# Hedgehog feature maps: min - x formed on GpSimd from x - max, and three value tiles with their constant columns set once

## The chip, the cores and the metric

The kernel runs on one core of a Trainium2 chip. The metric is the device time of one execution in microseconds (us); lower is better. The profile and the text use short names for the engines of the core: PE is TensorE (matmul), DVE is VectorE, ACT is ScalarE, POOL is GpSimd and SP is SyncE, which issues most DMAs.

## The reference

Four residual layers alternate, an ordinary attention (A) and a linear attention with "Hedgehog" features (B): A, B, A, B, on 2048 tokens of width 512, with 32 heads of 16. The part that matters here is B:

```python
pq = jnp.einsum("bhsd,hdf->bhsf", q, w_phi)
pk = jnp.einsum("bhsd,hdf->bhsf", k, w_phi)
phi_q = jnp.concatenate([_softmax(pq, axis=-1), _softmax(-pq, axis=-1)], axis=-1)
phi_k = jnp.concatenate([_softmax(pk, axis=-1), _softmax(-pk, axis=-1)], axis=-1)
kv = jnp.einsum("bhsf,bhsd->bhfd", phi_k, v)
z  = jnp.einsum("bhsf->bhf", phi_k)
num = jnp.einsum("bhqf,bhfd->bhqd", phi_q, kv)
den = jnp.einsum("bhqf,bhf->bhq", phi_q, z)[..., None] + 1e-6
o = num / den
```

For each token and head there are two softmaxes over 16 numbers, one of x and one of -x. A softmax of x is computed from x - max, one of -x from min - x.

## The kernel before, in words

The two A layers (`LayerA`) run their attention as one long sequence of PE, ACT and PE steps: scores (L877), exp (L880) and the product with the values (L891). Other work is put between them by a hand-written schedule (`pump`), in pieces of a generator.

The two B layers (`LayerB`) begin with `feed`, which goes over the 2048 tokens in 16 tiles of 128: `feed(j, ...)` is called for j = 0 to 3 and does four tiles each time; tt counts the tiles from 0 to 15. For each tile PE projects k's features into a PSUM bank (`pk`), q's into another (`pq`), and the values into a third (`pbv`), with 12 matmuls each (L1064). Three banks of the pool `psS` are there; one holds the sum of phi_k times v (`kvp`), so the three projections of a tile share two banks in turn, and each has to wait until the readers of the bank before it are done.

The steps of a tile after the projections, in the order in which the code issues them:

- `expo(pk)`: max (L1124) and min (L1125) over 16 numbers on DVE, then x - max (L1127) and min - x (L1128) on DVE into the two sides of `f`, 128 x 1024 numbers, then one exp on ACT (L1129). `expo(pq)` does the same for q.
- the values are copied to the high part of `vt` on ACT (L1097);
- `share` of k: the sums of 16 exps (L1135), the reciprocal (L1136) and a scale (L1138) on DVE, then the product on POOL (L1144); the low part of the values on DVE (L1092); `share` of q: L1135, L1136 and L1144, without a scale;
- `halves` of k: a high part in f16 on ACT (L1150), the low part on POOL (L1151).

Two things are done one tile later, in the middle of PE's projections of the next tile: `turn` transposes q's features on PE (L1175), and ACT copies them out (L1176); `gather` multiplies phi_k with the values on PE (L1182). The value tile `vt` holds, for two parts and 32 heads, 16 values and a seventeenth column with a constant: 1 in the high part, which makes the normalizer z, and 0 in the low part. It comes from a pool of five buffers (`yn`), and two memsets on POOL (L1068, L1069) set the constant columns for each tile.

During the first tiles `between` (a call to `pumps`) lets leftovers of the A layer run: the output projection of the last block of tokens (L585, L573), its layer statistics (L389 to L423, of which L396 and L397 are on DVE and L406 to L423, fourteen short steps, on POOL) and its transposition (L446 to L459). The memset L710 prepares a row for the next attention.

The order on all four compute engines in `feed` is the order of the code: it runs under `tc.manual_schedule(engines=COMPUTE)`, and each engine takes its instructions in that order. A wait at the head of an engine's queue holds up everything behind it. The last tile (tt = 15) goes another way at its end (`share_split`, `blocks`), and `rest` and `finish` follow with the outputs of the layer.

Of the kernel before, what the change touches and what calls it, by code (L numbers as in the profile page):

```python
# [10 lines left out]
F16 = mybir.dt.float16  # L11
# [3 lines left out]
ALU = mybir.AluOpType  # L15
AX = mybir.AxisListType

P = 128
S = 2048
D = 512  # L20
H = 32
DH = 16
# [28 lines left out]
def mha_hedgehog_stack(ctx, tc, x_in, a_wqkv, a_wo, b_wqkv, b_wphi, b_wo, out, shmin=SHMIN):  # L51
    nc = tc.nc
# [7 lines left out]
    np_ = pool("np", bufs=2)  # L60
# [5 lines left out]
    def big(shape, dt, name):  # L66
        return bigp.tile(shape, dt, tag="big", name=name)
# [306 lines left out]
    class Norm:  # L374
# [83 lines left out]
        def low(self, t, n, ps):  # L458
            nc.vector.tensor_tensor(self.part(1, t, n), ps.rearrange("p u (c x) -> p c u x", c=NC4), self.part(0, t, n), ALU.subtract)  # L459
# [156 lines left out]
    class LayerA:  # L616
# [4 lines left out]
        def begin(self, w0=None):  # L621
            self.start_octet(0, w0 or self.octet_w(0))
# [173 lines left out]
        def feed(self, lns, work):  # L796

            for j, (a, b, c) in enumerate(work):
                ln = lns[j]
                self.xnT.append(ln.xnT)  # L800
                ln.turn01()
                a()
                ln.turn23()
                b()
                c()
                if j == 2:
                    self.head_norms(0)
                self.head(j)
                if j == 2:
                    self.next_w = self.octet_w(1)  # L810
                    self.load_head()
                if 0 < j < NJ - 1:
                    self.head_values(j - 1)
            self.feed_end()
# [220 lines left out]
    class LayerB:  # L1035
# [3 lines left out]
        def begin(self):  # L1039
            self.wqk = stgp.tile([P, 2, 2, NC4, 512], F16, tag="stg", name="wbqk")  # L1040
            nc.sync.dma_start(self.wqk, dBqk)
            self.wv = []
            for a in range(2):
                t = wp.tile([P, NC4, 512], F16, tag="w", name=f"wbv{a}")
                nc.sync.dma_start(t, dBv[a])
                self.wv.append(t)
            self.kvp = None
            self.latek = self.lateq = None
            self.qT, self.obs = [], []

        def feed(self, j, xnT, between=lambda t: None):

            if self.kvp is None:
                self.kvp = psS.tile([P, 2, 512], F32, tag="S", name="kvp")
            qT = [big([P, 4, 512], F32, f"qT{j}_{i}") for i in range(2)]
            self.qT.append(qT)
            for t in range(4):
                tt = 4 * j + t

                def project(dst, w, passes=(0, 1, 2)):  # L1060
                    for i in passes:
                        a, b = PASSES[i]
                        for c in range(NC4):
                            nc.tensor.matmul(dst, xnT[:, a, c, t * P:(t + 1) * P], w(b, c),  # L1064
                                             start=(i == 0 and c == 0), stop=(i == 2 and c == NC4 - 1))

                vt = np_.tile([P, 2, H, 17], F16, tag="yn", name="vt", bufs=5)
                nc.gpsimd.memset(vt[:, 0, :, 16:17], 1.0)  # L1068
                nc.gpsimd.memset(vt[:, 1, :, 16:17], 0.0)  # L1069
                bank = lambda name: psS.tile([P, 2, 512], F32, tag="S", name=name)[:, 0, :]  # L1070
                last = tt == NT - 1
                pk = bank("pk")
                project(pk, lambda b, c: self.wqk[:, 1, b, c, :])
                if last:
                    f_k = self.expo(pk)
                    self.kvb = [np_.tile([P, 4, P], F32, tag="yn", name="kvb", bufs=5) for _ in range(2)]
                    for kvb in self.kvb:
                        nc.gpsimd.memset(kvb, 0.0)
                else:
                    pq = bank("pq")  # L1080
                    project(pq, lambda b, c: self.wqk[:, 0, b, c, :])
                if self.lateq is not None and tt < NT - 2:
                    self.turn(*self.lateq)
                pv_ = bank("pbv")
                project(pv_, lambda b, c: self.wv[b][:, c, :])
                if self.latek is not None:
                    self.gather(*self.latek)
                if last:
                    pq = bank("pq")
                    project(pq, lambda b, c: self.wqk[:, 0, b, c, :], (0, 1))  # L1090
                pvh = pv_.rearrange("p (h d) -> p h d", d=DH)
                low = lambda: nc.vector.scalar_tensor_tensor(  # L1092
                    vt[:, 1, :, 0:16], pvh, 2.0 ** -8, vt[:, 0, :, 0:16], op0=ALU.mult, op1=ALU.subtract)
                if not last:
                    f_k = self.expo(pk)
                    f_q = self.expo(pq)
                nc.scalar.activation(vt[:, 0, :, 0:16], pvh, AF.Copy, scale=2.0 ** -8)  # L1097
                if last:
                    fk = self.share_split(f_k, low)
                    self.turn(*self.todo)  # L1100
                    self.gather(tt, fk, vt)
                    project(pq, lambda b, c: self.wqk[:, 0, b, c, :], (2,))
                    self.blocks()
                    self.todo = [self.lateq, (tt, self.expo(pq), qT)]
                    for q in self.todo:
                        self.share(q[1], 1.0)
                    return
                self.share(f_k, KS)
                low()
                if tt == NT - 2:  # L1110
                    self.todo = self.lateq
                    self.latek = (tt, self.halves(f_k), vt)
                else:
                    self.share(f_q, 1.0)
                    self.latek = (tt, self.halves(f_k), vt)
                self.lateq = (tt, f_q, qT)
                between(tt)

        def expo(self, ps):

            pf = ps.rearrange("p (h f) -> p h f", f=DH)
            mx = sp.tile([P, H], F32, name="mx")
            mn = sp.tile([P, H], F32, name="mn")
            nc.vector.tensor_reduce(mx, pf, AX.X, ALU.max)  # L1124
            nc.vector.tensor_reduce(mn, pf, AX.X, ALU.min)  # L1125
            f = pp.tile([P, H, 2, DH], F32, tag="p", name="f")
            nc.vector.tensor_tensor(f[:, :, 0, :], pf, mx.unsqueeze(2).to_broadcast([P, H, DH]), ALU.subtract)  # L1127
            nc.vector.tensor_tensor(f[:, :, 1, :], mn.unsqueeze(2).to_broadcast([P, H, DH]), pf, ALU.subtract)  # L1128
            nc.scalar.activation(f, f, AF.Exp, scale=con["pB"])  # L1129
            return f  # L1130

# [270 lines left out]
```

## Time and profile before

| | us |
|---|---|
| median of 3 runs | 2550.31 |
| lowest and highest of them | 2549.44, 2551.63 |
| the profiled execution | 2549.26 |
| its span, from the first to the last instruction | 2547.5 |

| engine | busy us | share of the span | instructions |
|---|---|---|---|
| PE | 2447.8 | 96% | 20960 |
| DVE | 974.0 | 38% | 1884 |
| ACT | 2177.5 | 85% | 2437 |
| POOL | 379.0 | 15% | 523 |

The shares are means over very different stages. The feature stage of the first B layer lies at about 1043 to 1215 us of the span and that of the second at about 2293 to 2465 us; between them and before them lie the two attention layers. The granted PE clock was 0.99 over the span.

In the rows of the profile, a group of instructions has its source line, the engine, the operation, what it writes and reads, and how often it occurs; behind the bar stand its busy time, the mean ns of one, and the idle time of its engine in front of it with what ended that. Rows in order of time start with the start and the duration in us; a bracket at the end gives the idle time before the first instruction of the row and what ended it.

### The profile page before, as it was taken

What the parts mean: (1) busy time and instruction counts of PE and PEld (TensorE: products, weight loads), DVE (VectorE), ACT (ScalarE), POOL (GpSimd) and SP (SyncE); (2) the same over time, 40 slices, a digit from 0 to 9 for tenths busy, and PEclk for the clock granted to TensorE, in tenths of its full rate; (3) what the DMA queues carried; (4) which work ended last, traced back from release to release, by engine and by line L of the source; (5) the groups of instructions that cost most, each with busy time, mean ns of one, the idle gap of its engine ahead of it and who ended that gap; (6) DMA issues with size and microseconds to landing.
All of it is one profiled execution on the core that took longest, in us unless ns stands there. A gap on an engine that the chain in (4) does not pass through costs nothing.

```text
span 2547.5 us, 50724 instructions
## 1 busy us (share of the span) xinstructions
PE 2447.8 (96%) x20960; PEld 761.2 (30%) x20960; DVE 974.0 (38%) x1884; ACT 2177.5 (85%) x2437; POOL 379.0 (15%) x523
## 2 busy tenths in 40 slices
PE   6799999999999999999899999999999999998998
PEld 3222222222232222345343222222222222224543
DVE  6212211212133316899871122112122111459897
ACT  5699999999999999644438999999999999993552
POOL 2100000101000000266430010000010000005552
PEclk9899999999999999999999999999999999999999
DMA  3510230033033612100224003202300351110003
GB/s 141 104 44 5 43 47 6 14 50 78 1 79 66 222 51 84 50 17 6 70 96 68 14 6 50 40 1 45 65 2 10 71 140 41 67 67 26 9 17 109
DMA packets 109650, 135.29 MB, mean 53 GB/s; under 512 B 63408, under 2 KB 64672, under 8 KB 107232
## 3 DMA queue, kind: packets, MB, share of 16 engines
q1 hardware_dynamic: 108736, 129.59, 20.7%
q8 instruction: 166, 2.72, 0.4%
q0 software_dynamic: 672, 2.36, 0.2%
q14 instruction: 76, 0.62, 0.1%
HBM read 60.06 MB, written 39.85 MB: 39 GB/s over the span
## 4 chain that ended last, share of the span: by engine, by line
PE 78%; DVE 11%; ACT 5%; issue 3%; POOL 2%; SPq 1%; DMA 0%; ACTq 0%; POOLq 0%; DVEq 0%
PE pv L891 37%; PE s L877 21%; PE pqk L585 6%; PE po L585 5%; ACT p L880 3%; DVE su L1135 2%; PE pbv L1064 1%; PE pk L1064 1%; PE pq L1064 1%; DVE f L1127 1%; POOL f L1144 1%; DVE f L1128 1%; DVE mx L1124 1%; PE pst L446 1%; DVE su L1136 1%
## 5 line engine op out<-in xcount | busy, mean ns | idle before, releaser
L880 ACT ACTIVATE p<-s 128x1024 f32<-128x1024 f32 x2048 | 1887.8, 1116 | 20.2 <-PE s L877 17.7
L891 PE MATMUL pv<-p,v 128*32 128x512 f32 x8192 | 1091.9, 605 | 2.6 <-DVE yt L503 1.8
L877 PE MATMUL s<-kq 49*128 49x512 f16 x3872 | 606.1, 382 | 20.3 <-DMA kq<-sh 12.0
L877 PEld LDWEIGHTS <-kq 49*128 49x128 f16 x3968 | 136.8, 94 | 637.4 <-issue 625.3
L891 PEld LDWEIGHTS pv<-p,v 128*32 128x32 f32 x8192 | 161.8, 108 | 397.3 <-issue 367.2
L687 POOL TENSOR_TENSOR sq<-stg 128x512 bf16<-128x512 f16 x48 | 70.1, 1460 | 1043.1 <-DVE stg L761 940.2
L503 DVE STREAM_TRANSPOSE yt<-pv 128x512 f32<-128x512 f32 x64 | 45.8, 716 | 452.9 <-PE pv L891 441.0
L760 DVE TENSOR_SCALAR tq<-pqk,c_qk 128x512 f32<-128x512 f32 x48 | 35.9, 749 | 445.0 <-PE pqk L585 411.8
L1144 POOL TENSOR_TENSOR f<-f,su 128x1024 f32<-128x1024 f32 x62 | 119.8, 1933 | 386.0 <-DVE su L1138 351.6
L1064 PEld LDWEIGHTS <-xnTa 128*128 128x128 f16 x1152 | 110.6, 99 | 150.8 <-DVE f L1128 23.6
L585 PEld LDWEIGHTS <-wA 128*32 128x32 f16 (+1 forms) x2496 | 86.6, 97 | 200.8 <-issue 175.2
L573 DVE SCALAR_TENSOR_TENSOR xt<-po,c_oA,xt 128x512 f32<-128x512 f32 x64 | 47.1, 735 | 233.9 <-PE po L585 223.5
L585 PE MATMUL pqk<-xnTb,wA 128*32 128x512 f16 (+1 forms) x1248 | 116.9, 379 | 2.2 <-ACT xnTb L456 2.2
L585 PE MATMUL pqk<-xnT,wA 128*32 128x512 f16 (+1 forms) x1224 | 110.9, 379 | 3.1 <-ACT xnT L456 2.5
L1064 PE MATMUL pbv<-wbv,xnTa 128*128 128x512 f16 x384 | 92.9, 394 | 19.0 <-DVE f L1128 19.0
L1129 ACT ACTIVATE f<-f,c_pB 128x1024 f32<-128x1024 f32 x64 | 72.7, 1148 | 42.3 <-DVE f L1128 42.2
L1150 ACT ACTIVATE fk<-f 128x1024 f16<-128x1024 f32 x30 | 31.7, 1057 | 73.6 <-POOL f L1144 73.6
L585 PE MATMUL po<-woA,ob 128*32 128x512 f16 x1152 | 92.3, 379 | 0.0
L1064 PE MATMUL pk<-wbqk,xnTa 128*128 128x512 f16 x384 | 88.5, 379 | 0.0
L1064 PE MATMUL pq<-wbqk,xnTa 128*128 128x512 f16 x384 | 88.4, 379 | 0.0
L1135 DVE TENSOR_REDUCE su<-f 128x64 f32<-128x1024 f32 x64 | 77.5, 1211 | 9.2 <-ACT f L1129 8.5
L1176 ACT ACTIVATE qT<-pqt 128x512 f32<-128x512 f32 x64 | 34.6, 593 | 52.0 <-PE pqt L1175 52.0
(280 smaller groups left out, 1930.1 us busy)
## 6 DMA issues: line engine op xcount, KB each, us to landing
kq<-stg SPq DMA_DIRECT2D x168, 128.0 KB
xd<-xt SPq DMA_DIRECT2D x40, 512.0 KB
xt<-xd SPq DMA_DIRECT2D x40, 512.0 KB
v<-vyt SPq DMA_DIRECT2D x384, 16.0 KB
oD<-osp SPq DMA_DIRECT2D x24, 256.0 KB
ob<-oD SPq DMA_DIRECT2D x8, 768.0 KB
xt<-in_A_x_dram SPq DMA_DIRECT2D x8, 512.0 KB
wbqk<-dBqk SPq DMA_DIRECT2D x2, 2048.0 KB
```

The source lines that it names most:

```text
L503: nc.vector.transpose(yt.rearrange("p a b -> p (a b)"), ps)
L573: nc.vector.scalar_tensor_tensor(xt[:, u, :], ps, co, xt[:, u, :], op0=ALU.mult, op1=ALU.add)
L585: nc.tensor.matmul(ps[r, :], w[:, r], x, start=(n == 0), stop=(n == of - 1), skip_group_check=cols)
L687: nc.gpsimd.tensor_tensor(sq, hi, hi, ALU.mult)
L760: nc.vector.tensor_scalar(tq, ps, cqk, CLAMP, op0=ALU.mult, op1=ALU.min)
L877: nc.tensor.matmul(s[:, u, :], self.side(g, half, r, 0, kt * P, P), self.side(g, half, r, 1, j * 512, 512), start=True, stop=True)
L880: nc.scalar.activation(pt, s, AF.Exp, scale=0.25 / (QS * QS))
L891: nc.tensor.matmul(acc[32 * hh:32 * hh + 32, :], self.oct[o]["v"][:, r:r + 32], pt[:, hh % 2, :], start=(kt == 0), stop=(kt == NT - 1), sk ...
L1064: nc.tensor.matmul(dst, xnT[:, a, c, t * P:(t + 1) * P], w(b, c), start=(i == 0 and c == 0), stop=(i == 2 and c == NC4 - 1))
L1129: nc.scalar.activation(f, f, AF.Exp, scale=con["pB"])
L1135: nc.vector.tensor_reduce(su, f[:, r, :], AX.X, ALU.add)
L1144: nc.gpsimd.tensor_tensor(f3, f3, self.part_sums(f3, slice(0, 64), factor), ALU.mult)
```

## The change

In `expo`, the step min - x no longer reads PSUM on DVE. POOL first forms min - max (32 numbers per partition) and then (min - max) - (x - max), which is min - x, from the side of `f` that DVE has just written. DVE keeps max, min and x - max. In `feed`, three value tiles are made in the first three tiles of tokens, with the constant columns set there, and used in turn by the others.

```diff
-            self.qT, self.obs = [], []
+            self.qT, self.obs, self.vts = [], [], []
...
-                vt = np_.tile([P, 2, H, 17], F16, tag="yn", name="vt", bufs=5)
-                nc.gpsimd.memset(vt[:, 0, :, 16:17], 1.0)
-                nc.gpsimd.memset(vt[:, 1, :, 16:17], 0.0)
+                if tt < 3:
+                    self.vts.append(np_.tile([P, 2, H, 17], F16, tag="yn", name="vt", bufs=5))
+                    nc.gpsimd.memset(self.vts[tt][:, 0, :, 16:17], 1.0)
+                    nc.gpsimd.memset(self.vts[tt][:, 1, :, 16:17], 0.0)
+                vt = self.vts[tt % 3]
...
             nc.vector.tensor_tensor(f[:, :, 0, :], pf, mx.unsqueeze(2).to_broadcast([P, H, DH]), ALU.subtract)
-            nc.vector.tensor_tensor(f[:, :, 1, :], mn.unsqueeze(2).to_broadcast([P, H, DH]), pf, ALU.subtract)
+            nc.gpsimd.tensor_tensor(mn, mn, mx, ALU.subtract)
+            nc.gpsimd.tensor_tensor(f[:, :, 1, :], mn.unsqueeze(2).to_broadcast([P, H, DH]), f[:, :, 0, :], ALU.subtract)
             nc.scalar.activation(f, f, AF.Exp, scale=con["pB"])
```

## The prediction

> **What bounds the kernel now.** I read the page from the top: the engines' shares, then the chain that ended last, then the feature stage alone, first in stretches and then instruction by instruction.
>
> ```profile
> span 2547.5 us, 50724 instructions
> PE 2447.8 (96%) x20960; PEld 761.2 (30%) x20960; DVE 974.0 (38%) x1884; ACT 2177.5 (85%) x2437; POOL 379.0 (15%) x523
> PE pv L891 37%; PE s L877 21%; PE pqk L585 6%; PE po L585 5%; ACT p L880 3%; DVE su L1135 2%; PE pbv L1064 1%; PE pk L1064 1%; PE pq L1064 1%; DVE f L1127 1%; POOL f L1144 1%; DVE f L1128 1%; DVE mx L1124 1%; PE pst L446 1%; DVE su L1136 1%
> ```
>
> TensorE carries the whole kernel, and L891 and L877 of the chain, its two attention layers, hold none of the changed lines. VectorE (DVE; L1135, L1127, L1128, L1124) and GpSimd (POOL; L1144) reach the chain only in the feature stage, which runs twice, over 16 tiles of 128 tokens each time. So I look there. Two stretches of it, one with side work (a tile with leftovers of the attention layer) and one quiet; columns are PE, weight loads, DVE, ACT, POOL busy time, clock, DMA share and GB/s:
>
> ```profile
> 1142.00:1153.00 11.00, 10.03 (x72) 5.59 (x72) 9.52 (x16) 5.31 (x8) 6.16 (x6) 1.00 0.01 1
> 1182.20:1191.60 9.40, 9.40 (x69) 5.13 (x68) 9.08 (x15) 4.78 (x7) 6.29 (x6) 1.00 0.01 2
> ```
>
> In the quiet tile PE is busy for 9.40 of 9.40 us; DVE is close to full; POOL has 3.1 us free. In the other tile nobody is full. The order in time says why. A quiet tile (k and q are the two halves of a tile's features):
>
> ```profile
> 1179.07 1.93 POOL L1144 TENSOR_TENSOR f<-f,su 128x1024 f32<-128x1024 f32 x1 [0.40 <-DVE su L1136]
> 1180.96 2.14 POOL L1151 TENSOR_TENSOR fk<-f,fk 128x1024 f16<-128x1024 f32 x1
> 1181.16 1.04 PE L1175 MATMUL pqt<-ident,f 128*128 128x128 f32 x8
> 1181.80 1.08 ACT L1176 ACTIVATE qT<-pqt 128x512 f32<-128x512 f32 x2 [2.03 <-PE pqt L1175]
> 1182.77 2.26 ACT L1129 ACTIVATE f<-f,c_pB 128x1024 f32<-128x1024 f32 x2
> 1183.95 1.22 DVE L1135 TENSOR_REDUCE su<-f 128x64 f32<-128x1024 f32 x1
> 1186.13 1.94 POOL L1144 TENSOR_TENSOR f<-f,su 128x1024 f32<-128x1024 f32 x1 [2.71 <-DVE su L1138]
> 1188.47 1.94 POOL L1144 TENSOR_TENSOR f<-f,su 128x1024 f32<-128x1024 f32 x1 [0.40 <-DVE su L1136]
> 1190.36 2.13 POOL L1151 TENSOR_TENSOR fk<-f,fk 128x1024 f16<-128x1024 f32 x1
> ```
>
> This is a ring from one q share on POOL (1179.07, L1144) to the next (1188.47), 9.40 us. The share's end (1181.00) lets PE transpose it (L1175), ACT copies the transposes out (L1176), and only behind them in ACT's queue stands the next tile's exp of k (1182.77); then the sums (L1135) and k's share, q's sums and q's share. The PE transposes start when PE has finished its projection, so PE and this ring are both nearly tight. Note POOL at 1180.96: it forms the low part of k (L1151) right behind q's share, until 1183.10, and its reader, PE's gather, comes later still.
>
> A tile with side work has pieces of both layers on DVE:
>
> ```profile
> 1142.47 2.76 PE L1064 MATMUL pbv<-wbv,xnTa 128*128 128x512 f16 x12 [1.07 <-DVE f L1128]
> 1153.58 2.76 PE L1064 MATMUL pbv<-wbv,xnTa 128*128 128x512 f16 x12 [1.07 <-DVE f L1128]
> ```
>
> Its period is 11.11 us, and PE waits 1.07 us for DVE's L1128, the last reader of the PSUM bank that PE wants.
>
> **The change, part by part.** The prices first: POOL's rows, the DVE row that goes, and two DVE steps that follow one another.
>
> ```profile
> L1144 POOL TENSOR_TENSOR f<-f,su 128x1024 f32<-128x1024 f32 x62 | 119.8, 1933 | 386.0 <-DVE su L1138 351.6 <-DVE su L1136 28.5 <-PE po L585 5.9
> L687 POOL TENSOR_TENSOR sq<-stg 128x512 bf16<-128x512 f16 x48 | 70.1, 1460 | 1043.1 <-DVE stg L761 940.2 <-DVE rec L505 102.9
> L523 POOL TENSOR_TENSOR obB<-yb,obB 128x512 f16<-128x512 f32 x32 | 37.2, 1162 | 68.2 <-ACT obB L522 68.2
> L1069 POOL MEMSET vt<- 128x32 f16 x32 | 10.3, 321 | 0.0
> L1068 POOL MEMSET vt<- 128x32 f16 x32 | 7.6, 239 | 98.3 <-DVE yb L518 98.3
> L710 POOL MEMSET sh<- 1x512 f16 x12 | 6.2, 514 | 175.4 <-PE po L585 161.2 <-DMA kqe<-sh 11.4 <-DMA kq<-sh 2.8
> L1128 DVE TENSOR_TENSOR f<-mn,pk 128x512 f32<-128x512 f32 x16 | 10.8, 677 | 0.0
> 1189.37 0.68 DVE L1127 TENSOR_TENSOR f<-pk,mx 128x512 f32<-128x512 f32 x1
> 1189.96 0.68 DVE L1128 TENSOR_TENSOR f<-mn,pk 128x512 f32<-128x512 f32 x1
> ```
>
> Removed from DVE: one L1128 per half, 64 in all. It lasts 677 ns, but consecutive steps start 0.59 us apart (1189.37, 1189.96), so a tile's two halves free 1.2 us of DVE. The bank of PSUM is also freed 0.6 us sooner. The constant columns: 52 of the 64 memsets (239 and 321 ns) go; they lie in POOL's idle time, nobody waits for them, so by themselves they are worth nothing. The reuse of three value tiles adds no wait that matters: tile t writes a buffer whose last reader, the gather of tile t-3, ran two tiles earlier.
>
> Added on POOL, per half: a 128x32 subtraction, and a 128x512 f32 subtraction. No row shows the latter. From below it is half of L1144's 1933 ns, 0.97 us; from above L687's 1.46 us, which has the element count but 16-bit types; L523 has 1.16. I take 1.06: L1144 is the same type and engine, and 0.19 us of it, the time of a nearly empty POOL step (1070.86, next fence), does not halve: (1.93 - 0.19)/2 + 0.19. The Trainium skill's "GPSIMD Engine Reference", section 3.1, has 4497 ns for a two-input f32 step of 2048 elements, so by estimate 1.12 for 512; the sum would grow by 1.7 us. Section 4.1 of that page of the Trainium skill speaks against the change outright: elementwise two-input work belongs on VectorE, GpSimd being about twice as slow; the rows here agree (1.06 by 0.68). For the small one I look at POOL's short steps behind a statistics step:
>
> ```profile
> 1068.63 2.13 POOL L1151 TENSOR_TENSOR fk<-f,fk 128x1024 f16<-128x1024 f32 x1
> 1068.79 2.00 DVE L397 TENSOR_SCALAR ly<-lu 128x2 int32<-128x2 int32 x1
> 1070.86 0.19 POOL L406 TENSOR_TENSOR lu<-ly 128x2 f32<-128x2 f32 x1
> 1074.39 0.20 POOL L423 TENSOR_TENSOR lb<-lu,ly 128x2 f32<-128x2 f32 x1
> ```
>
> From L406 to L423 are 14 short steps, each waiting for the one before: 3.53/13 = 0.27 us a step. That is the small subtraction's price (128x2 here, 128x32 there; 0.27 to 0.33). The same fence shows an oddity: L397, a two-column DVE step, took 2.00 us and ended as POOL's L1151 did (1070.79 and 1070.76). The Trainium skill's "GPSIMD Engine Reference", section 8, says that the two engines share their SBUF interfaces and contend when DVE runs in a two-port mode or has two SBUF inputs; this row agrees. In a quiet tile the one DVE step of L397's kind (a number times a column in SBUF) is the scaling of k's sums, for which POOL will stand idle, so no term follows from it; in front of the statistics L397 ends with the low part before and after the change.
>
> What decides is where POOL's new work stands. In the changed program POOL's order per tile is: small and large subtraction of k, of q, then k's share, q's share, k's low part. GpSimd takes them in that order. So tile t+1's subtraction of k is queued behind q's share and k's low part of tile t, and ACT's exp, DVE's sums, k's share wait behind it. The low part, which held nobody up, enters the ring:
>
> q's share to the low part's start 1190.36 - 1188.47 = 1.89; low part 2.13; small 0.27; large 1.06; to ACT 0.04; exp of k to the next q share 1188.47 - 1182.77 = 5.70. Sum 11.09 us per tile, against 9.40 in a quiet tile and 11.11 in one with side work. PE's own 9.40 fits under it; DVE's 1.2 us become idle time in front of L1135.
>
> Now one layer, from q's share of tile 0 to that of tile 9 and of tile 13:
>
> ```profile
> 1057.14 1.93 POOL L1144 TENSOR_TENSOR f<-f,su 128x1024 f32<-128x1024 f32 x1 [0.36 <-DVE su L1136]
> 1160.34 1.93 POOL L1144 TENSOR_TENSOR f<-f,su 128x1024 f32<-128x1024 f32 x1 [0.40 <-DVE su L1136]
> 1197.86 1.94 POOL L1144 TENSOR_TENSOR f<-f,su 128x1024 f32<-128x1024 f32 x1 [0.40 <-DVE su L1136]
> 1204.71 1.93 POOL L1144 TENSOR_TENSOR f<-f,su 128x1024 f32<-128x1024 f32 x1 [2.52 <-DVE su L1138]
> 1207.81 2.13 POOL L1151 TENSOR_TENSOR fk<-f,fk 128x1024 f16<-128x1024 f32 x1 [1.17 <-ACT fk L1150]
> 1208.74 1.15 ACT L1129 ACTIVATE f<-f,c_pB 128x1024 f32<-128x1024 f32 x1 [1.01 <-DVE f L1128]
> ```
>
> The first nine periods take 103.20 us, the last four 37.52 (9.38 each). After: four quiet ones are 44.36, so +6.8. The first nine are 99.8, plus what POOL must do in between: twice the statistics (3.53 + 0.20 = 3.73, ahead of k's subtraction in the queue), two pairs of memsets that stay (0.24 + 0.32 each; the third pair runs before the stage), and one L710 (0.51): 108.9, so +5.7. Tile 14's k share then stands 5.39 + (1186.13 - 1182.77 = 3.36) = 8.75 behind q's share of tile 13 instead of 6.85: +1.9. In tile 15 the exp (1208.74) would wait for the low part of tile 14 (until 1209.94) and the two subtractions: 1209.94 + 0.27 + 1.06 + 0.04 = 1211.31, +2.6; part of it is covered by PE's projection and the gather behind it, and in the stage behind, where DVE ends last, the last L1128 gives back 0.6. I take half of 2.6 less 0.6, +0.7, of 0 to 2.6. Per layer 6.8 + 5.7 + 1.9 + 0.7 = 15.1; twice, as both layers run the same program, 30.2.
>
> The profiled execution took 2549.26 us, 1.8 more than its span, and 1.05 less than the median of 2550.31. 2549.26 + 30.2 + 1.05 = 2580.5: I forecast 2580.
>
> **The rivals.** *Faster, 2532 us.* By sums POOL has room: 6.29 busy of 9.40, plus 2 x 1.33, less 0.56 of memsets, is 8.4. Were the new steps hidden so, DVE's 1.2 us would count where PE waits for L1128 (1.07 us in the tile with side work): nine tiles, twice, 1.0 each, -18. It holds if k's subtraction gets onto POOL before tile t-1's low part. The queue's order says no; it would take shares that finish earlier than now, and the q share is itself at the end of the DVE work. 5%.
>
> *No change, 2550.* The early tiles gain what the quiet ones lose: 6.8 a layer over nine tiles, 0.75 each. It needs the ring to be 10.3 us where there is side work, so a subtraction at 0.3 us; nothing in the rows is that cheap. 3%.
>
> *Dearer, 2591 to 2602.* The large step reads and writes every other run of 16 numbers, and could cost like L687, 1.46. The ring grows by 0.40 per tile if only k's step is in it: 28 x 0.40 = 11, 2591; up to 22, 2602, if q's step delays its exp and through ACT's queue the low step of the values. 12%.
>
> **How the numbers follow.** The likeliest case has 80%. Its lower end takes 0.97 for the large step (-0.09 in each of 14 periods a layer, -2.5) and nothing for tile 15 (-1.4), 2576; a little more for a ring that closes tighter than my sum, 2570. The upper end takes most of the dearer case, 2600. A measurement of this kernel can tell some 0.2%, 5 us, from no change. Slower by more than that is 92%, within it 3%, faster 5%.
>
> **What would show it.** In the changed profile quiet tiles should have q shares 11.1 us apart; ACT's exp should be released by POOL, not DVE; PE should wait for POOL or for DVE's sums; DVE's idle time in front of L1135 should grow; the new 128x512 row should read 1.0 to 1.2 us; POOL should be nearly without gaps from q's share to the next subtraction of k. I am wrong if quiet tiles stay at 9.4 us, or if exp starts before the low part of the tile before has ended.

## The result and the profile after

The changed kernel takes 2586.05 us (median of 4 runs, 2584.79 to 2588.74), the kernel before in the same session 2549.88 (4 runs, 2547.28 to 2551.63): 36.2 us more, a ratio of 1.0144 [1.0132, 1.0156]. The forecast was 2580, with a range of 2570 to 2600. The profiled execution took 2586.64, its span 2584.9.

I read the page again from the top. The span, the engines and the chain that ended last, of the changed kernel (the last line is the chain's, by engine and line):

```profile
span 2584.9 us, 50771 instructions
PE 2458.9 (95%) x20960; PEld 763.1 (30%) x20960; DVE 937.7 (36%) x1820; ACT 2181.8 (84%) x2437; POOL 451.9 (17%) x599
PE pv L891 37%; PE s L877 20%; PE pqk L585 5%; PE po L585 5%; ACT p L880 3%; DVE su L1138 3%; POOL f L1147 2%; POOL fk L1154 2%; ACT f L1132 1%; DVE su L1139 1%; POOL f L1131 1%; PE pn L1207 1%; PE pst L446 1%; DVE vt L1094 1%; DVE st L389 1%
```

DVE has 36.3 us less to do and POOL 72.9 more, 64 + 64 steps against 52 memsets fewer. The chain now names POOL three times: L1147 (the share; L1144 before, then 1%), L1154 (the low part of k; L1151 before, not in the list then) and the new L1131.

The prices, from the groups of POOL's instructions (count, then busy time and mean ns of one, then the idle time before and who ended it):

```profile
L1131 POOL TENSOR_TENSOR f<-mn,f 128x512 f32<-128x512 f32 x64 | 67.7, 1058 | 7.2 <-DVE f L1129 2.5
L1130 POOL TENSOR_TENSOR mn<-mn,mx 128x32 f32<-128x32 f32 x64 | 16.2, 253 | 258.0 <-DVE mn L1127 257.7
```

The large step takes 1058 ns where 1.06 us was forecast, the small one 253 ns. Now a quiet tile, in order of time, from one q share on POOL to the next:

```profile
1177.10 1.93 POOL L1147 TENSOR_TENSOR f<-f,su 128x1024 f32<-128x1024 f32 x1 [0.38 <-DVE su L1139]
1178.99 2.14 POOL L1154 TENSOR_TENSOR fk<-f,fk 128x1024 f16<-128x1024 f32 x1
1179.09 1.09 PE L1178 MATMUL pqt<-ident,f 128*128 128x128 f32 x8 [1.04 <-POOL f L1147]
1181.08 0.25 POOL L1130 TENSOR_TENSOR mn<-mn,mx 128x32 f32<-128x32 f32 x1
1181.41 1.06 POOL L1131 TENSOR_TENSOR f<-mn,f 128x512 f32<-128x512 f32 x1
1182.50 1.15 ACT L1132 ACTIVATE f<-f,c_pB 128x1024 f32<-128x1024 f32 x1 [1.64 <-POOL f L1131]
1183.69 1.22 DVE L1138 TENSOR_REDUCE su<-f 128x64 f32<-128x1024 f32 x1 [3.20 <-ACT f L1132]
1185.87 1.94 POOL L1147 TENSOR_TENSOR f<-f,su 128x1024 f32<-128x1024 f32 x1 [2.05 <-DVE su L1141]
1188.18 1.93 POOL L1147 TENSOR_TENSOR f<-f,su 128x1024 f32<-128x1024 f32 x1 [0.37 <-DVE su L1139]
```

1188.18 - 1177.10 = 11.08 us, against 9.40 before. POOL runs without a gap from q's share (1177.10) through the low part (1178.99), the small step (1181.08) and the large one (1181.41); ACT's exp of k waits 1.64 us for exactly that last step, and DVE's sums wait 3.20 us for the exp where they came without a wait before. POOL has its only long gap, 2.05 us, in front of k's share (1185.87), where it stands waiting for DVE. PE waits 1.04 us for the q share (1179.09). The same period in PE, weight loads, DVE, ACT and POOL busy time, clock, DMA share, GB/s:

```profile
1177.10:1188.18 11.08, 9.77 (x70) 5.09 (x69) 7.77 (x13) 4.92 (x7) 8.50 (x8) 1.00 0.00 1
```

PE is no longer full in a quiet tile (9.77 of 11.08), DVE has 7.77 and POOL 8.50. No engine is full: the loop over the four engines is the bound. So every sign that the prediction named is there.

How much of the 36 us lies where is read from the share rows, here those at which the sections of a layer begin and end (tile 0's k share and q share, the q shares of tiles 9 and 13, tile 14's k share, the last share; then the first and last of the second layer), first after, then those of before that have not been shown:

```profile
1054.70 1.94 POOL L1147 TENSOR_TENSOR f<-f,su 128x1024 f32<-128x1024 f32 x1 [1.51 <-DVE su L1141]
1057.44 1.93 POOL L1147 TENSOR_TENSOR f<-f,su 128x1024 f32<-128x1024 f32 x1 [0.80 <-DVE su L1139]
1166.01 1.93 POOL L1147 TENSOR_TENSOR f<-f,su 128x1024 f32<-128x1024 f32 x1 [0.38 <-DVE su L1139]
1210.34 1.93 POOL L1147 TENSOR_TENSOR f<-f,su 128x1024 f32<-128x1024 f32 x1 [0.38 <-DVE su L1139]
1219.11 1.93 POOL L1147 TENSOR_TENSOR f<-f,su 128x1024 f32<-128x1024 f32 x1 [2.05 <-DVE su L1141]
1243.01 1.93 POOL L1147 TENSOR_TENSOR f<-f,su 128x1024 f32<-128x1024 f32 x1 [1.77 <-DVE su L1139]
2323.67 1.94 POOL L1147 TENSOR_TENSOR f<-f,su 128x1024 f32<-128x1024 f32 x1 [1.51 <-DVE su L1141]
2512.18 1.93 POOL L1147 TENSOR_TENSOR f<-f,su 128x1024 f32<-128x1024 f32 x1 [1.77 <-DVE su L1139]
```

```profile
1054.84 1.94 POOL L1144 TENSOR_TENSOR f<-f,su 128x1024 f32<-128x1024 f32 x1 [18.50 <-DVE su L1138]
1225.82 1.93 POOL L1144 TENSOR_TENSOR f<-f,su 128x1024 f32<-128x1024 f32 x1 [1.78 <-DVE su L1136]
2304.80 1.93 POOL L1144 TENSOR_TENSOR f<-f,su 128x1024 f32<-128x1024 f32 x1 [242.72 <-DVE su L1138]
2474.79 1.93 POOL L1144 TENSOR_TENSOR f<-f,su 128x1024 f32<-128x1024 f32 x1 [1.78 <-DVE su L1136]
```

| part of a layer, us | before, layer 1 / 2 | after, layer 1 / 2 | difference | forecast |
|---|---|---|---|---|
| k share to q share of tile 0 | 2.30 / 2.30 | 2.74 / 2.75 | +0.44 / +0.45 | none |
| first nine periods | 103.20 / 102.20 | 108.57 / 108.54 | +5.37 / +6.34 | +5.7 |
| last four periods | 37.52 / 37.52 | 44.33 / 44.32 | +6.81 / +6.80 | +6.8 |
| to tile 14's k share | 6.85 / 6.86 | 8.77 / 8.77 | +1.92 / +1.91 | +1.9 |
| from there to the last share | 21.11 / 21.11 | 23.90 / 24.13 | +2.79 / +3.02 | +0.7 |
| the layer | 170.98 / 169.99 | 188.31 / 188.51 | +17.33 / +18.52 | +15.1 |

The two layers hold 35.85 of the 37.4 us by which the spans differ. Of the rest, 1.68 lie between the layers, where nothing changed; over the kernels below, this stretch varies between 1078.3 and 1082.3 us without any order that follows the edits, so I don't put it down to the change.

### The profile page after: what moved, and what is told of

It reads as the page before. It is cut to its first block, busy times and chain, and to the rows that moved or that the text cites. A ratio compares the mean times of both kernels' runs of the same rounds, so it can differ in the third digit from the quotient of the medians.

```text
span 2584.9 us, 50771 instructions
## 1 busy us (share of the span) xinstructions
PE 2458.9 (95%) x20960; PEld 763.1 (30%) x20960; DVE 937.7 (36%) x1820; ACT 2181.8 (84%) x2437; POOL 451.9 (17%) x599
## 4 chain that ended last, share of the span: by engine, by line
PE 73%; DVE 11%; POOL 6%; ACT 6%; issue 3%; SPq 1%; DMA 0%; POOLq 0%; ACTq 0%; DVEq 0%
PE pv L891 37%; PE s L877 20%; PE pqk L585 5%; PE po L585 5%; ACT p L880 3%; DVE su L1138 3%; POOL f L1147 2%; POOL fk L1154 2%; ACT f L1132 1%; DVE su L1139 1%; POOL f L1131 1%; PE pn L1207 1%; PE pst L446 1%; DVE vt L1094 1%; DVE st L389 1%
## 5 line engine op out<-in xcount | busy, mean ns | idle before, releaser
L1147 POOL TENSOR_TENSOR f<-f,su 128x1024 f32<-128x1024 f32 x62 | 119.9, 1933 | 80.0 <-DVE su L1141 62.4
L1138 DVE TENSOR_REDUCE su<-f 128x64 f32<-128x1024 f32 x64 | 77.6, 1213 | 83.0 <-ACT f L1132 83.0
L1153 ACT ACTIVATE fk<-f 128x1024 f16<-128x1024 f32 x30 | 31.7, 1058 | 70.1 <-POOL f L1147 70.1
L585 PE MATMUL po<-wbo,obB 128*128 128x512 f16 x336 | 75.7, 385 | 3.3 <-DVE xnTb L459 3.3
```

The lines of the kernel that those rows point to most:

```text
L585: nc.tensor.matmul(ps[r, :], w[:, r], x, start=(n == 0), stop=(n == of - 1), skip_group_check=cols)
L1138: nc.vector.tensor_reduce(su, f[:, r, :], AX.X, ALU.add)
L1147: nc.gpsimd.tensor_tensor(f3, f3, self.part_sums(f3, slice(0, 64), factor), ALU.mult)
```

## The experiments

Two theories went into the experiments. T1, from the prediction: the order of POOL's queue costs the time; q's share and k's low part now stand in front of the next tile's subtraction of k, and so in the ring. T2: it is the sum of POOL's work (1.3 us per half), wherever in the queue it stands. All ratios are to the kernel before, timed on the same chip (2549.45, 2548.95 and 2549.85 us in the three sessions: E1 to E4, E5 to E8, E9 to E12).

### E1 and E2: the same spare step at two places

A spare 128x512 f32 step on POOL, whose output nobody reads, once per tile: in E1 behind k's low part, in E2 in the gap in front of k's share.

```diff
 # E1
                     self.latek = (tt, self.halves(f_k), vt)
+                    self.spare()
 # E2
+                if not last:
+                    self.spare()
                 self.share(f_k, KS)
 # both
+        def spare(self):
+            junk = np_.tile([P, 4, P], F32, tag="yt", name="junk", bufs=3)
+            one = ident.unsqueeze(1).to_broadcast([P, 4, P])
+            nc.gpsimd.tensor_tensor(junk, one, one, ALU.subtract)
```

> The changed kernel with one more 128x512 f32 step on POOL in tiles 0 to 13, whose result nobody reads, queued behind k's low part and ahead of the next tile's subtraction of k. Theory 1, the place in POOL's queue: the stretch from q's share to the next subtraction of k is part of the ring that sets the tile's period, so the step costs its full 1.06 us in 14 tiles of 2 layers, +30 us on the changed kernel, 2614 to 2618, with q's shares 12.1 us apart in quiet tiles. Theory 2, the amount of work on POOL (or POOL and DVE holding one another up): also about +30. Rival of both, POOL has slack there: 2586.

> The same step added in tiles 0 to 14, but queued in front of k's share, where POOL stands idle for 2.05 us until DVE has scaled k's sums. Theory 1, the place in the queue: nothing, 2584 to 2588, q's shares 11.1 us apart, and POOL's idle time in front of k's share down by 1.1 us. Theory 2, the amount of POOL's work or its contention with DVE: like the kernel with the step in the ring, about 2616; half of it if contention alone.

E1 took 2610.86 us (2610.25 to 2612.65), ratio 1.0240 [1.0223, 1.0257], 24.8 more than the changed kernel. E2 took 2583.89 (2583.12 to 2584.25), ratio 1.0134 [1.0117, 1.0151], 2.2 less. In order of time, E1:

```profile
1185.78 1.93 POOL L1148 TENSOR_TENSOR f<-f,su 128x1024 f32<-128x1024 f32 x1 [0.38 <-DVE su L1140]
1189.77 1.04 POOL L1154 TENSOR_TENSOR junk<-ident 128x512 f32<-128x512 f32 x1
1197.86 1.93 POOL L1148 TENSOR_TENSOR f<-f,su 128x1024 f32<-128x1024 f32 x1 [0.38 <-DVE su L1140]
```

The spare step (L1154) starts at 1189.77, behind the low part, and the q shares (L1148) are 12.08 us apart, 1.00 more than 11.08, for a step of 1.04. The two layers, from the first share to the last, are 27.5 us longer (201.25 + 203.11 against 188.31 + 188.51), about 1 us for each of 28 periods; the medians differ by 24.8, so the time was some 3 us under what both theories had said. E2:

```profile
1184.01 1.04 POOL L1155 TENSOR_TENSOR junk<-ident 128x512 f32<-128x512 f32 x1
1186.11 1.93 POOL L1149 TENSOR_TENSOR f<-f,su 128x1024 f32<-128x1024 f32 x1 [1.05 <-DVE su L1143]
1188.42 1.93 POOL L1149 TENSOR_TENSOR f<-f,su 128x1024 f32<-128x1024 f32 x1 [0.38 <-DVE su L1141]
1199.49 1.93 POOL L1149 TENSOR_TENSOR f<-f,su 128x1024 f32<-128x1024 f32 x1 [0.38 <-DVE su L1141]
```

The same step (L1155) stands at 1184.01, the gap behind it shrinks from 2.05 to 1.05, and the q shares (L1149) are 11.07 us apart. The same work costs 25 us in one place and nothing in the other. T2 falls.

### E3 and E4: the memsets

E3 is the changed kernel with the value tile and its two memsets made for each tile, as before. E4 is the kernel before with only the value tiles of the change.

```diff
 # E3, on the changed kernel
-                if tt < 3:
-                    self.vts.append(np_.tile([P, 2, H, 17], F16, tag="yn", name="vt", bufs=5))
...
-                vt = self.vts[tt % 3]
+                vt = np_.tile([P, 2, H, 17], F16, tag="yn", name="vt", bufs=5)
+                nc.gpsimd.memset(vt[:, 0, :, 16:17], 1.0)
+                nc.gpsimd.memset(vt[:, 1, :, 16:17], 0.0)
 # E4, on the changed kernel: the step min - x as before
-            nc.gpsimd.tensor_tensor(mn, mn, mx, ALU.subtract)
-            nc.gpsimd.tensor_tensor(f[:, :, 1, :], mn.unsqueeze(2).to_broadcast([P, H, DH]), f[:, :, 0, :], ALU.subtract)
+            nc.vector.tensor_tensor(f[:, :, 1, :], mn.unsqueeze(2).to_broadcast([P, H, DH]), pf, ALU.subtract)
```

> Only the first part of the change: min - x on POOL, but a fresh value tile with two memsets for each tile of tokens, as in the kernel before. Theory 1: the memsets now stand on POOL in the ring, ahead of the subtraction of k; 0.44 to 0.56 us in 12 tiles of 2 layers, 2597 to 2600. Theory 2, or memsets that nobody waits for as before the change: 2586.

> Only the second part of the change: three value tiles with their columns set once, min - x on DVE as before. Both theories: the memsets lay in POOL's idle time, so 2548 to 2552. Rival: the reuse of the three tiles adds a wait, or a shorter POOL queue frees the shares earlier: outside of 2545 to 2555.

E4: 2550.79 us (2549.86 to 2553.49), ratio 1.0008 [0.9998, 1.0017]: setting the columns once is worth nothing by itself, as the prediction said. E3: 2590.26 (2588.89 to 2591.05), ratio 1.0158 [1.0141, 1.0175], 4.2 more than the changed kernel. Both theories missed, mine by size. Its queue:

```profile
1182.36 0.24 POOL L1068 MEMSET vt<- 128x32 f16 x1
1182.41 0.32 POOL L1069 MEMSET vt<- 128x32 f16 x1
1182.50 0.27 POOL L1128 TENSOR_TENSOR mn<-mn,mx 128x32 f32<-128x32 f32 x1
1189.61 1.93 POOL L1145 TENSOR_TENSOR f<-f,su 128x1024 f32<-128x1024 f32 x1 [0.38 <-DVE su L1137]
1200.80 1.93 POOL L1145 TENSOR_TENSOR f<-f,su 128x1024 f32<-128x1024 f32 x1 [0.38 <-DVE su L1137]
```

The memsets (L1068, L1069) are in the ring, but the second starts 0.05 us after the first and the next step 0.14 us after the first, though the rows give them 0.24 and 0.32: they overlap. The q shares (L1145) are 11.19 us apart, 0.11 more than 11.08, instead of the 0.56 that I had summed. So the memsets do join the ring once POOL sets its pace, and there the pair costs 0.11 to 0.14 us, some 4 us over the kernel.

### E5 and E6: k's half alone and q's half alone

```diff
-        def expo(self, ps):
+        def expo(self, ps, pool=False):
...
+            if pool:
+                nc.gpsimd.tensor_tensor(mn, mn, mx, ALU.subtract)
+                nc.gpsimd.tensor_tensor(f[:, :, 1, :], mn.unsqueeze(2).to_broadcast([P, H, DH]), f[:, :, 0, :], ALU.subtract)
+            else:
+                nc.vector.tensor_tensor(f[:, :, 1, :], mn.unsqueeze(2).to_broadcast([P, H, DH]), pf, ALU.subtract)
 # E5
-                    f_k = self.expo(pk)
+                    f_k = self.expo(pk, True)
 # E6
-                    f_q = self.expo(pq)
+                    f_q = self.expo(pq, True)
```

> Only k's min - x on POOL (tiles 0 to 14), q's on DVE, columns set once. Theory 1, the place in the queue: k's subtraction behind the low part is the whole ring, so nearly all of the loss stays: quiet tiles 11.1 us, 2573 to 2581 (the last tile, on DVE here, gives back 2 to 3 us a layer). Theory 2, the amount of POOL's work: half the loss, 2566 to 2570.

> Only q's min - x on POOL (tiles 0 to 14), k's on DVE, columns set once. Theory 1: k's exp no longer waits for POOL; q's exp comes some 0.6 us later than before and holds up the values' copy behind it on ACT and so DVE's low part, so quiet tiles 9.4 to 9.7 us, tiles with side work 0.6 shorter: 2546 to 2555. Theory 2, the amount: half the loss, 2566 to 2570.

E5: 2579.87 us (2576.41 to 2580.93), ratio 1.0121 [1.0105, 1.0136]. E6: 2554.24 (2552.97 to 2557.25), ratio 1.0021 [1.0011, 1.0030]. Both leave tile 15 as it was before. k's half costs 30.9 us and q's half alone 5.3; by T2 the two would have cost alike. E6 sits at the upper end of what T1 allowed. Its trace:

```profile
1175.19 1.15 ACT L1135 ACTIVATE f<-f,c_pB 128x1024 f32<-128x1024 f32 x1 [0.59 <-POOL f L1132]
1176.86 0.69 DVE L1094 SCALAR_TENSOR_TENSOR vt<-pbv,vt 128x512 f16<-128x512 f32 x1 [0.19 <-ACT vt L1099]
```

ACT waits 0.59 us for POOL's step of q before its exp (L1135). Behind that exp in ACT's queue is the copy of the values (L1099), and DVE's low part of the values (L1094) waits 0.19 us for the copy. Quiet q shares are 9.62 us apart (9.40 before); in E5 they are 11.10.

### E7: the last tile as before

```diff
                 if last:
-                    f_k = self.expo(pk)
+                    f_k = self.expo(pk, False)
...
-                    self.todo = [self.lateq, (tt, self.expo(pq), qT)]
+                    self.todo = [self.lateq, (tt, self.expo(pq, False), qT)]
```

> The changed kernel, but with min - x of the last tile (k and q) on DVE as before. Tests the term of the sum that was too small, tile 15: if the exp of that tile waits in full for the low part and the subtractions, and nothing behind it gives any of it back, 2.6 to 2.9 us a layer return: 2580 to 2581. If that part was covered as the prediction took it (0.7 a layer): 2584 to 2585.

2578.14 us (2576.39 to 2580.22), ratio 1.0119 [1.0103, 1.0134]: 7.9 less than the changed kernel, or 7.0 when each is taken against the kernel before of its own session; either is more than the two readings had. The section from tile 14's k share to the last share is 21.26 and 20.06 us, against 23.90 and 24.13, so 2.64 and 4.07 come back there, 6.7 in all. Tile 15 is where the prediction fell short. That more came back than was lost has a reason in the trace. With the step on DVE, the exp of k in the last tile starts 2.93 us behind tile 14's k share (1217.89 to 1220.82, and the same in the second layer); in the changed kernel it is 6.60 and in the kernel before 4.03. In the kernel before, DVE's maximum of tile 15 waits 1.06 us for PE's projection (1206.22); in E7 the slower ring has let PE finish it early. So the step on POOL delays that exp by 3.7 us, and the 2.6 to 2.9 had counted from the kernel before. The first layer of E7 shows less of it, as its granted clock was 0.63 from 1224.13 to 1228.20. What is left, 29.2 us over the 2548.95 of its session, is the price of both halves in tiles 0 to 14, and E5 has 30.9 for k's half in the same tiles: on top of k's half, q's costs nothing. The 30.9 and 5.3 of E5 and E6 make up the 36.2 of the change by chance only; tile 15 is in neither.

### E8 and E11: the copy of the values ahead of q's exp

E8 is E6 with one line of ACT moved; E11 moves it in the kernel before.

```diff
                     f_k = self.expo(pk)
-                    f_q = self.expo(pq)
                 nc.scalar.activation(vt[:, 0, :, 0:16], pvh, AF.Copy, scale=2.0 ** -8)
+                if not last:
+                    f_q = self.expo(pq, True)     # E11: self.expo(pq)
```

> Only q's min - x on POOL, and ACT copies the values' high part before q's exp and not behind it, so that DVE's low part of the values does not wait for POOL. Theory 1: quiet tiles stay at PE's 9.4 us, tiles with side work get 0.6 us shorter as DVE is relieved and the bank of q's projection frees sooner: 2540 to 2546, below both kernels. Theory 2, the amount of POOL's work: half the loss, 2566 to 2570.

> The kernel before (min - x on DVE, memsets for each tile) with one edit: ACT copies the values ahead of q's exp. Control for the run with q's min - x on POOL and the values first: if its gain comes from POOL's relief of DVE, this one stays at 2547 to 2552; if from the order on ACT alone, 2542 to 2546.

E8: 2544.47 us (2542.68 to 2546.60), ratio 0.9981 [0.9972, 0.9990]. E11: 2549.67 (2547.40 to 2553.01), ratio 1.0000 [0.9991, 1.0009]. E8's ACT:

```profile
1172.85 0.60 ACT L1098 ACTIVATE vt<-pbv 128x512 f16<-128x512 f32 x1 [0.91 <-PE pbv L1064]
1173.34 1.14 ACT L1136 ACTIVATE f<-f,c_pB 128x1024 f32<-128x1024 f32 x1
```

The copy (L1098) now stands in front of q's exp (L1136), which then finds POOL's step done and waits for nothing. Quiet q shares are 9.39 us apart, as before, and those with side work 10.5 instead of 11.1, as DVE has 0.6 us less to do per tile. Moving one half of the step off DVE does pay, 4.5 us, if POOL's part stands behind the low part in a place where it holds nobody up. E11 shows that the order on ACT alone is worth nothing.

### E9 and E10: the changed kernel with the low part elsewhere

Both halves on POOL, as many steps as in the change; only k's low part is issued later. In E9 it goes behind the next tile's subtraction of k, in E10 behind both subtractions; PE's gather, which reads it, moves along, and E9 has ACT's copy ahead of q's exp as E8 has.

```diff
-            nc.gpsimd.tensor_tensor(fk[:, 1, :], ff, fk[:, 0, :], ALU.subtract)
+            self.lowk = lambda: nc.gpsimd.tensor_tensor(fk[:, 1, :], ff, fk[:, 0, :], ALU.subtract)
...
                     f_k = self.expo(pk)
+                    # E9: self.lowk() and self.gather(*self.latek) here
+                    # E9: the copy of the values here
                     f_q = self.expo(pq)
+                    # E10: self.lowk() and self.gather(*self.latek) here
```

> The changed kernel with the same steps on POOL in another order: k's low part is issued one tile later, between the next tile's subtraction of k and that of q, and ACT copies the values ahead of q's exp. Theory 1, the place in the queue: the ring is q's share to k's subtraction 1.89, the subtractions 0.33 + 1.06, to ACT 0.04, exp of k to q's share 5.70, together 9.02 us, below PE's 9.40; q's subtraction, now the one behind the low part, costs some tenths. Quiet tiles 9.4 to 9.8 us, 2545 to 2556: nearly the whole loss returns with no step less on POOL. Theory 2, the amount of POOL's work or contention: 2584 to 2588.

> The changed kernel with k's low part issued one tile later, behind both subtractions of the next tile. Theory 1: k's exp comes early again, but now PE's gather waits for the low part, which ends 1.89 + 2 x 1.37 + 2.13 = 6.8 us after q's share began, and PE's projections behind it; quiet tiles 11.1 to 11.4 us, 2578 to 2590, and the gather's wait in place of the exp's. Theory 2: 2584 to 2588, with no wait of the gather.

E9: 2557.84 us (2556.00 to 2560.51), ratio 1.0032 [1.0022, 1.0043]. Without a step less on POOL, 28.2 of the 36.2 us come back. T2 had 2584 to 2588 here; T1 holds, although the time is 2 us over what it had allowed. The move of ACT's copy is part of the 28.2, and E9 without it wasn't run. Its queue:

```profile
1180.42 2.13 POOL L1160 TENSOR_TENSOR fk<-f,fk 128x1024 f16<-128x1024 f32 x1
1182.84 1.05 POOL L1137 TENSOR_TENSOR f<-mn,f 128x512 f32<-128x512 f32 x1
1183.93 1.15 ACT L1138 ACTIVATE f<-f,c_pB 128x1024 f32<-128x1024 f32 x1 [0.43 <-POOL f L1137]
```

The low part (L1160) is now in front of q's subtraction (L1137), so q's exp (L1138) waits 0.43 us for that; quiet q shares are 9.88 us apart. The copy's move is needed for this, by an estimate from these rows. Behind q's exp (1183.93) the copy would start 1.06 us later, as in the changed kernel (1183.85 to 1184.91), DVE's low part of the values would start at about 1185.60 and not at 1183.97, and q's sums 1.1 us later than they do. Quiet periods would then be about 11.0 us, and most of the loss would stay. In the changed kernel, on the other hand, that low part waits for nothing in a quiet tile (1185.64), so the copy's move alone should bring nothing there. E9 thus shows what the order on POOL and ACT does together; neither part alone was measured. E10: 2596.42 (2595.31 to 2597.27), ratio 1.0181 [1.0166, 1.0197], slower than the change itself and 6 us over the upper end of what T1 gave for this place:

```profile
1174.82 2.13 POOL L1159 TENSOR_TENSOR fk<-f,fk 128x1024 f16<-128x1024 f32 x1
1176.20 0.80 DVE L1146 TENSOR_SCALAR su<-su 128x64 f32<-128x64 f32 x1
1177.00 0.89 PE L1190 MATMUL kvp<-vt,fk 128*128 128x68 f16 x23 [1.78 <-POOL fk L1159]
```

The low part (L1159) is now so late that PE's gather (L1190), and with it the next projection in PE's queue, waits 1.78 us for it. Nor does DVE's scale in the second row pass it by, of which more below. Quiet periods are 11.34 us. A late place in the queue is thus no gain in itself: the low part belongs where its own reader has not yet come and the ring is not held up.

### E12: q's half in the last tile too

```diff
 # on E8
-                    self.todo = [self.lateq, (tt, self.expo(pq), qT)]
+                    self.todo = [self.lateq, (tt, self.expo(pq, True), qT)]
```

> q's min - x on POOL in all 16 tiles, k's on DVE, the values first. In the last tile of a layer DVE ends last, so its step moved to POOL gives back about 0.6 us a layer against the run where that tile stays on DVE: 2541 to 2545. Rival: q's exp of that tile is late instead, up to 0.7 us a layer more: 2545 to 2548.

2544.76 us (2542.02 to 2547.28), ratio 0.9974 [0.9963, 0.9985]. The section from tile 14's k share to the last share is 21.36 us, against 21.70 in E8: 0.34 a layer, less than the 0.6 of the DVE step. E8 and E12 can't be told apart by their times; both beat the kernel before, by 4.5 and 5.1 us by the medians of their sessions, and the changed kernel by over 41.

| kernel | us | ratio to before | quiet period, us |
|---|---|---|---|
| before | 2549.88 | 1 | 9.40 |
| the change | 2586.05 | 1.0144 [1.0132, 1.0156] | 11.08 |
| E5, k's half only | 2579.87 | 1.0121 [1.0105, 1.0136] | 11.10 |
| E6, q's half only | 2554.24 | 1.0021 [1.0011, 1.0030] | 9.62 |
| E8, E6 with the values' copy first | 2544.47 | 0.9981 [0.9972, 0.9990] | 9.39 |
| E9, the change, low part between, values' copy first | 2557.84 | 1.0032 [1.0022, 1.0043] | 9.88 |
| E10, the change, low part behind both | 2596.42 | 1.0181 [1.0166, 1.0197] | 11.34 |

## Why the prediction was right, and where it was short

**The queue's order: right, and shown.** The step on which all hung was that POOL takes the next tile's subtraction of k behind q's share and k's low part. The trace shows this order without a gap, and E9 shows that order, and not the amount of work, is the cost: the same steps on every engine, only in another order on POOL, PE and ACT, bring 28 of 36 us back. E1 and E2 show it for POOL's queue alone, with a step that the kernel doesn't need.

**The ring and its terms: right.** 11.08 us measured for 11.09 forecast; the large step 1058 ns for 1.06 us. By starts of the rows above: to the low part 1.89 (forecast 1.89), to the small step 2.09 (2.13), to the large one 0.33 (0.27), to ACT's exp 1.09 (1.06 + 0.04), to the next q share 5.68 (5.70). The four quiet periods are 44.33 for 44.36, tile 14's k share 8.77 for 8.75 behind, the nine periods 108.57 and 108.54 for 108.9. That the nine periods came so close is in part luck, as errors in their side work cancel. In the first layer two terms were too dear: the two pairs of memsets cost 0.27 us of the 1.12 that I had put in, and L710 cost 0.04 of 0.51, as it falls into POOL's wait for q's sums. The two statistics took 3.83 and 3.79 us instead of 3.73. And 0.91 us had no term: behind the first statistics ACT has side work (L433) and its copies ahead of k's exp, which starts 0.9 us after POOL's step is done (1077.99 and 1078.94).

**The first nine periods of the second layer: 0.6 short.** I had taken the kernel before from its first layer. Its second layer took 102.20 us there, 1.0 less. The same stretch of the two layers of the kernel before (the second begins 1249.96 us later):

```profile
1097.00:1109.00 12.00, 10.20 (x64) 5.05 (x65) 11.04 (x18) 3.95 (x4) 7.48 (x17) 0.86 0.00 0
2347.00:2359.00 12.00, 10.17 (x71) 5.41 (x72) 11.90 (x20) 4.62 (x6) 7.99 (x17) 1.00 0.00 0
```

The granted clock was 0.86 in the first layer's and 1.00 in the second's. After the change POOL's ring sets the pace, and both layers take 108.5. So the second layer lost 6.34 and the first 5.37.

**Tile 15: the term that was mis-sized.** I took +0.7 of 0 to 2.6; it measured +2.79 and +3.02. In order of time in the changed kernel:

```profile
1222.21 2.12 POOL L1154 TENSOR_TENSOR fk<-f,fk 128x1024 f16<-128x1024 f32 x1 [1.17 <-ACT fk L1153]
1224.39 0.89 PE L1185 MATMUL kvp<-vt,fk 128*128 128x68 f16 x23 [1.99 <-POOL fk L1154]
1225.71 1.15 ACT L1132 ACTIVATE f<-f,c_pB 128x1024 f32<-128x1024 f32 x1 [3.58 <-POOL f L1131]
1228.96 0.83 DVE L1164 TENSOR_TENSOR f<-f,su 128x640 f32<-128x640 f32 x1
1232.83 1.76 PE L1064 MATMUL pq<-wbqk,xnTa 128*128 128x512 f16 x4
1234.63 0.69 DVE L1126 TENSOR_REDUCE mx<-pq 128x32 f32<-128x512 f32 x1 [0.56 <-PE pq L1064]
```

The exp is released by POOL after 3.58 us of waiting, as in the fully exposed case of the prediction, and DVE starts the split share (L1164) 9.85 us behind tile 14's k share. In the kernel before this was 7.28 (L1161, next row, from 1204.71):

```profile
1211.99 0.83 DVE L1161 TENSOR_TENSOR f<-f,su 128x640 f32<-128x640 f32 x1
```

That is +2.57 (+2.58 in the second layer), the whole of the 2.6 that I had halved. PE's projection and the gather, which I had named as its cover, cover nothing: the gather (L1185) itself waits 1.99 us for the low part. Half of a bound without a row that shows the cover was a guess; E7 confirms the place.

The 0.6 that the last L1128 was to give back did come back, in the first layer in full. From DVE's maximum of q's numbers (L1126; L1124 before) to the last share it is 8.38 and 8.55 us, against 8.98 (1216.84 to 1225.82) and 8.99 in the kernel before. It doesn't show in the sum, because that maximum comes later behind the split share: 5.67 and 5.72 us instead of 4.85 and 4.84. It waits for PE, whose last four matmuls of q's projection took 1.76 and 1.90 us instead of 1.03 (1215.59 before). The granted clock in the 3 us around them was 0.61 in the first layer (from 1232.00) and 0.50 in the second (from 2501.00); in the kernel before it was 1.00 from the split share to the last share in both layers. The prediction had no term for this, and why the clock was lower there stays open. So 2.57 - 0.60 + 0.82 make the 2.79 of the first layer, and 2.58 - 0.44 + 0.88 the 3.02 of the second.

**What else was missed: 0.44 a layer** from tile 0's k share to its q share. It is the chain of E6 once more: q's exp waits 0.73 us for POOL, the copy of the values stands behind it on ACT, and DVE's low part of the values, with q's sums behind it, waits 0.33:

```profile
1053.22 1.15 ACT L1132 ACTIVATE f<-f,c_pB 128x1024 f32<-128x1024 f32 x1 [0.73 <-POOL f L1131]
1054.89 0.69 DVE L1094 SCALAR_TENSOR_TENSOR vt<-pbv,vt 128x512 f16<-128x512 f32 x1 [0.33 <-ACT vt L1099]
```

I had no term for it. The forecast of 30.2 us, and 4.4 for tile 15, 0.9 for tile 0, 0.3 for the nine periods, make 35.8 of the 35.85 measured in the two layers.

**The rivals.** "Faster" would have needed the subtraction of k ahead of the low part; it isn't. E8 shows its mechanism alive for q's half: 0.6 us of DVE per tile is worth 4.5 us where DVE holds PE up. "No change" would have needed a ring of 10.3 us. "Dearer" had a step of 1.46 us; it is 1058 ns. Its second thought, q's step delaying its exp and through ACT the low part of the values, is real in E6, where taking it away (E8) is worth 9.8 us, and in tile 0; in the ring of the changed kernel it costs nothing (E7 against E5, and 11.08 against 11.10 us a quiet tile).

The page of the Trainium skill that the prediction weighed against the trace, "GPSIMD Engine Reference", section 3.1, gave by estimate 1.12 us for the large step; 1058 ns was measured, so the row's own halving was nearer. Against DVE's 677 ns the step is 1.6 times as long on POOL, less than the "about twice" with which the prediction had said its rows agree.

## What to carry to other kernels

Before moving a step to an engine with idle time, write down that engine's queue around the new place: everything already queued ahead of the step joins the loop that waits for it, here 4.0 us of share and low part for a step of 1.06. Ask of each step in that queue who waits for it and when; half of the step moved off DVE was worth 4.5 us where it stood behind the low part and, with the copy moved, in front of nobody, and the other half cost 31. And take an exposed wait in a last tile at its full size, unless a row shows what runs beneath it.

## What the runs showed of the hardware

- Two memsets on POOL that follow one another overlap: rows of 0.24 and 0.32 us, but only 0.14 us from the first's start to the next instruction's (E3).
- A dependent POOL step starts 0.33 us after a small step of 253 ns (1181.08 to 1181.41), and an independent one 1.02 us after a large step of 1058 ns (1181.41 to 1182.43 in the changed kernel).
- DVE's scale of 64 sums (L1146 in E10) took 0.80 us instead of 0.20 and ended at 1177.00, as POOL's low part ended (1174.82 + 2.13 = 1176.95). It is the same kind of step as L397 in the prediction, which took 2.00 us and ended with a low part. L532 in the stage behind the features does the same in the kernel before: 1.06 us from 1223.03, to the end of POOL's share (1222.12 + 1.93), and 0.11 us at 1225.82. The Trainium skill's "GPSIMD Engine Reference", section 8, says that the two engines share their SBUF interfaces; the rows here show that this kind of DVE step may be held until POOL's instruction ends.
